# Three early attention jobs: the softmax denominator of rounds 1, 3 and 5 taken by the ones matmul from both key tiles, without the pair sum on VectorE

## The chip, the cores and the metric

The kernel runs on one core of a Trainium2 chip. The metric is the device time of one execution in microseconds (us). A core has a matrix engine (TensorE, PE in the profile; its weight loads are listed apart as PEld), VectorE (DVE), ScalarE (ACT), GpSimd (POOL) and a queue that issues the DMAs (SP). They run at the same time and wait for each other through semaphores. Each engine carries out its own instructions in the order of the program.

## What is computed

One transformer layer on 2048 tokens of width 1024, 32 heads of 32, and a feed-forward of width 3584, in bf16:

```python
scores = jnp.einsum("bhqd,bhkd->bhqk", q, k) * scale
p = _softmax(scores, axis=-1)
o = jnp.einsum("bhqk,bhkd->bhqd", p, v)
...
h = x + _A_ref(_layernorm(x, axis=-1), A_wqkv, A_wo)
h2 = h + _B_ref(_layernorm(h, axis=-1), B_w1, B_b1, B_w2, B_b2)
```

`_A_ref` is the attention with its projections, and `_B_ref` is the feed-forward with a tanh gelu. The change touches only the sum under the softmax, the denominator.

## The kernel before

**Jobs and rounds.** A job (class `Job`, L817) is 256 queries (`qb`, 0 to 7) of one group of four heads (`g`, 0 to 7), so there are 64 jobs. A job runs over the 2048 keys in eight rounds of two key tiles of 128. In each round, `qk` (L783) issues eight matmuls that put the scores of four heads and two key tiles into four PSUM banks (L796). ScalarE takes the exponential of them in two instructions of 128x1024 (L807) into a bf16 buffer `PT`. `pv` (L826) multiplies `PT` with `V` in eight matmuls (L833). These add into the first half of one PSUM bank that belongs to the job. No maximum is subtracted.

**The denominator.** It is made by a matmul with a matrix of ones, `den` (L856, matmuls at L862), which adds into the second half of the job's bank. In rounds 0 to 6, VectorE first adds the two key tiles of the round (L848, 128x1024) into a buffer `PS`, so that `den` has four matmuls. In round 7 the tile pair is taken directly: eight matmuls, and no add. There are three `PS` buffers (`NS = 3`), used in turn. An add writes a buffer only after the `den` that read it last. A `den` is issued after the `pv` of the next round. When a job is complete, `finish` (L870) has VectorE take both halves out of the bank (L878 and L885), and so frees the bank for the next taker.

**Banks.** PSUM has eight banks. Six serve the scores, in three units of two. The other two, 6 and 7, are handed out by the planner: each goes to an attention job, or to one background output (a projection or a feed-forward block) at a time. Background matmuls are recorded at L556, L559 and L562, and their results are taken out by VectorE (for instance L681, L733 and L752).

**The lead.** At the start, while tokens are still being normalized, transposed and projected, the kernel already runs scores and exponentials of three jobs, `qb` 0, 1 and 2 of head group 0 (`NLJ = 3`, L1078 to L1100). These are the lead jobs. Their 24 rounds go to buffers that stay filled: eight of the nine regular `PT` buffers and sixteen extra ones, `PX`, that lie in places that are used for something else later (K and V of other groups, and projection weights). Their `pv` and `den` come only when all keys and the V of group 0 are there. Their adds on VectorE wait for the last VectorE task of the lead (`after=hold`, L849). Background outputs that come after the key projections of group 1 wait for the end of that stage (`gate`, `late`).

**Order.** No order is written by hand. All work is put into a graph of tasks with costs, and a planner (`schedule`, L121) plays the execution forward and writes down each engine's order. On VectorE the ready task with the lowest priority number goes first: a pair sum has -2, the taking out of a finished job's bank has -1, and the taking out of a projection has 0. On TensorE (`pick_pe`, L1210) scores go first, then a closing `den`, then `pv` and `den` when enough rounds wait, and then background work. The planner counts 0.60 us for an add (`c_dve(1024, 2)`), 0.22 us for a direct `den` and 0.11 us for one from `PS`. The orders that it writes down are then fixed in the program, and the chip runs them with semaphores. A changed task can therefore alter the order of everything that is planned after it.

## Time and profile before

| | us |
|---|---|
| median of 3 runs | 1084.93 |
| lowest, highest | 1082.6, 1089.91 |
| the profiled execution | 1087.09 |
| its span in the profile | 1085.3 |
| TensorE busy (matmuls) | 1045.5 (96%) |
| ScalarE busy | 1014.5 (93%) |
| VectorE busy | 755.3 (70%) |
| exponentials into `PT`, L807, x992 | 924.5 |
| exponentials into `PX`, L807, x32 | 31.2 |
| pair sums, L848, x434 | 287.8 |
| ones matmuls from `PS`, L862, x1792 | 127.1 |

Matmuls overlap, so TensorE's busy time is not its share of peak. The mean duration of an instruction includes its pipeline. The distance from one start to the next is shorter, and is what counts when instructions follow one another without a gap. Numbers such as 62.49 in the rows are the start in us from the beginning of the span, and the second number is the time that the merged group took. Brackets behind a row give the idle time before it and who ended it.

### The profile page before, as it was taken

The numbers are of one execution on the slowest core, as the hardware profiler recorded it, in microseconds if no ns is written. First come the engines' busy times: TensorE is split into PE (matmuls) and PEld (weight loads), VectorE is DVE, ScalarE is ACT, GpSimd is POOL, SyncE is SP. The second block draws the span as 40 slices with busy tenths as digits, with TensorE's granted clock in tenths as the row PEclk, the third lists the DMA queues.
The fourth block names the chain that finished last, engine by engine and source line by source line (L and its number), as shares of the span: only waits on it lengthen the run. The fifth ranks groups of instructions, "written<-read, shape, count | busy, mean of one in ns | idle before, by whom it ended". The sixth has DMA issues, their size and how long they took to land.

```text
span 1085.3 us, 41670 instructions
## 1 busy us (share of the span) xinstructions
PE 1045.5 (96%) x18957; PEld 608.6 (56%) x19014; DVE 755.3 (70%) x1447; ACT 1014.5 (93%) x1116; POOL 43.2 (4%) x110
## 2 busy tenths in 40 slices
PE   8999999998899999999999999999999999899998
PEld 6566555554344754574475457447546744464483
DVE  8786666566586896698499669848966967686401
ACT  4999999999999999999999999999999999999650
POOL 4200000000010001001000100100010001000100
PEclk9999999999999999999999999999999999899999
DMA  8661444438464645654764565476466556866260
GB/s 221 168 163 35 145 143 120 137 118 291 161 171 147 200 164 193 231 179 147 260 220 159 206 232 177 149 258 217 159 209 233 176 191 209 248 226 236 77 244 20
DMA packets 136177, 196.37 MB, mean 181 GB/s; under 512 B 49216, under 2 KB 100288, under 8 KB 133184
## 3 DMA queue, kind: packets, MB, share of 16 engines
q1 hardware_dynamic: 136000, 193.70, 54.1%
q8 instruction: 149, 2.44, 0.9%
q14 instruction: 28, 0.23, 0.1%
HBM read 177.94 MB, written 27.26 MB: 189 GB/s over the span
## 4 chain that ended last, share of the span: by engine, by line
ACT 65%; PE 30%; DVE 3%; issue 1%; POOL 0%; POOLq 0%; DVEq 0%
ACT PT L807 60%; PE ps L559 8%; PE ps L562 6%; PE ps L556 6%; PE ps L796 4%; ACT uu L1014 3%; PE ps L833 3%; ACT PX L807 2%; PE ps L862 2%; DVE PS L848 1%; PE ps L1055 1%; PE ps L629 0%; DVE uu L1013 0%; ACT xnT L636 0%; DVE hch L1037 0%
## 5 line engine op out<-in xcount | busy, mean ns | idle before, releaser
L807 ACT ACTIVATE PT<-ps 128x1024 bf16<-128x1024 f32 x992 | 924.5, 1085 | 11.4 <-PE ps L796 10.5
L848 DVE TENSOR_TENSOR PS<-PT 128x1024 bf16<-128x1024 bf16 x434 | 287.8, 685 | 122.5 <-ACT PT L807 63.1
L796 PE MATMUL ps<-QT,KT 32*128 32x256 bf16 x4096 | 204.8, 274 | 8.0 <-ACT PT L807 6.3
L833 PE MATMUL ps<-PT,V 128*32 128x256 bf16 x3968 | 176.8, 274 | 3.4 <-ACT PT L807 3.2
L796 PEld LDWEIGHTS ps<-QT,KT 32*128 32x128 bf16 x4096 | 60.8, 92 | 162.4 <-ACT PT L807 135.9
L862 PE MATMUL ps<-PS,ones 128*32 128x256 bf16 x1792 | 127.1, 276 | 3.5 <-DVE PS L848 2.5
L559 PE MATMUL ps<-hnT,a_w1r 128*128 128x256 bf16 x979 | 119.1, 273 | 1.9 <-DVE hch L1037 1.1
L833 PEld LDWEIGHTS ps<-PT,V 128*32 128x32 bf16 x3968 | 102.1, 97 | 33.5 <-issue 6.7
L559 PEld LDWEIGHTS ps<-hnT,a_w1r 128*128 128x128 bf16 x979 | 90.1, 98 | 27.0 <-issue 15.9
L556 PE MATMUL ps<-a_w2r,gT 128*32 128x512 bf16 x1380 | 100.8, 381 | 0.6 <-DVE gT L1016 0.4
L559 PE MATMUL ps<-a_w2r,gT 128*128 128x512 bf16 x390 | 96.2, 380 | 2.8 <-issue 1.9
L556 PE MATMUL ps<-hnT,a_w1r 128*32 128x256 bf16 x2356 | 84.3, 275 | 3.3 <-issue 1.8
L992 DVE TENSOR_TENSOR gT<-ps,b1f 128x512 bf16<-128x512 f32 x98 | 67.3, 687 | 17.0 <-PE ps L559 8.9
L1037 DVE SCALAR_TENSOR_TENSOR hch<-ps,hch 128x512 bf16<-128x512 f32 x32 | 22.0, 688 | 72.3 <-PE ps L562 47.1
L556 PEld LDWEIGHTS ps<-hnT,a_w1r 128*32 128x32 bf16 x2356 | 58.6, 97 | 18.0 <-issue 15.9
L862 PEld LDWEIGHTS ps<-PS,ones 128*32 128x32 bf16 x1792 | 48.0, 97 | 28.5 <-DVE PS L848 10.2
L559 PEld LDWEIGHTS ps<-a_w2r,gT 128*128 128x128 bf16 x411 | 35.3, 98 | 46.9 <-issue 12.5
L559 PE MATMUL ps<-xnT,Wall 128*128 128x512 bf16 (+1 forms) x259 | 54.6, 344 | 2.3 <-issue 1.0
L1014 ACT ACTIVATE uu<-uu 128x1024 bf16<-128x1024 bf16 x49 | 55.3, 1129 | 0.0
L556 PEld LDWEIGHTS ps<-a_w2r,gT 128*32 128x32 bf16 x1380 | 30.5, 96 | 26.0 <-issue 16.2
L613 POOL CAST mvb<-mv 128x2 bf16<-128x2 f32 (+1 forms) x25 | 5.0, 210 | 983.1 <-DVE mv L610 983.1
L878 DVE STREAM_TRANSPOSE OD<-ps 128x256 f32<-128x256 f32 x64 | 28.5, 446 | 13.7 <-PE ps L862 6.7
(91 smaller groups left out, 1017.8 us busy)
## 6 DMA issues: line engine op xcount, KB each, us to landing
a_w2r<-w_blocks SPq DMA_DIRECT2D x105, 512.0 KB, 5.8
a_w1r<-w_blocks SPq DMA_DIRECT2D x98, 512.0 KB, 3.6
wov<-wo_blocks SPq DMA_DIRECT2D x16, 1024.0 KB, 4.9
w_blocks<-in_B_w_dram SPq DMA_DIRECT2D x28, 512.0 KB, 3.9
b_w1r<-w_blocks SPq DMA_DIRECT2D x14, 512.0 KB, 4.0
a_w1r<-in_A_wqkv_dram SPq DMA_DIRECT2D x11, 512.0 KB, 4.7
Wall<-in_A_wqkv_dram SPq DMA_DIRECT2D x17, 256.0 KB, 4.2
xrb<-in_A_x_dram SPq DMA_DIRECT2D x16, 256.0 KB, 4.8
```

The source lines that it names most:

```text
L556: fns.append(lambda p, j=j: p.matmul(psum[32 * j:32 * j + 32, bi(bank), c0:c1], lhsT[:, 32 * j:32 * j + 32], rhs, start=start, stop=stop, ...
L559: t.whole = lambda p: p.matmul(psum[:, bi(bank), c0:c1], lhsT, rhs, start=start, stop=stop, skip_group_check=True)
L562: t = pe(lambda p: p.matmul(psum[:, bi(bank), c0:c1], lhsT, rhs, start=start, stop=stop), occ, reads=reads, writes=[bb(bank)], mode="full" ...
L796: return p.matmul(psum[:, 2 * us[h // 2] + h % 2, 256 * i:256 * i + 256], KT[32 * h:32 * h + 32, g, k0:k0 + P], QT[32 * h:32 * h + 32, qs, :],
L807: act(lambda a, u=u, k=k: a.activation(PTs[s][:, k, :, :], psum[:, 2 * u:2 * u + 2, :], ACT.Exp, bias=0.0, scale=SCALE), 1024, reads=[B_ps ...
L833: fns.append(lambda p, i=i, h=h: p.matmul(psum[32 * h:32 * h + 32, bi(bank), 0:256], V[:, g, 2 * r + i, 32 * h:32 * h + 32], PTs[s][:, h / ...
L848: dve(lambda v: v.tensor_tensor(PS[:, n, :, :], pairs[:, :, 0:256], pairs[:, :, 256:512], ALU.add), c_dve(1024, 2), reads=B_PTs[s], writes ...
L862: fns.append(lambda p, h=h, rhs=rhs, i=i: p.matmul(psum[32 * h:32 * h + 32, bi(bank), 256:512], ones32[:, :], rhs, start=False, stop=last, ...
L878: t = dve(lambda v: v.transpose(OD[:, o, 1, :], psum[:, bi(bank), 256:512]), 0.36, reads=[self.B_O, self.B_D], writes=B_D, prio=-1)
L992: t = dve(lambda v: v.tensor_tensor(g[:, fc:fc + 2, :], psum[:, bi(bank), :].rearrange("p (f c) -> p f c", f=2), b1f[:, fc:fc + 2].unsquee ...
L1014: act(lambda a: a.activation(w, w, ACT.Tanh, bias=0.0, scale=KT2), 1024, reads=[B_uu[i]], writes=[B_uu[i]], prio=-1)
L1037: drop(dve(lambda v, hs=hs, bank=bank, half=half: v.scalar_tensor_tensor(hch[:, hs, c], psum[:, bi(bank), :], half, hch[:, hs, c], ALU.mul ...
```

## The change

In the three lead jobs, rounds 1, 3 and 5 are now treated as round 7 was: the round's buffer goes straight to `den`, which issues eight ones matmuls on its two tiles; no add is issued on VectorE and no `PS` buffer is taken for the round. All other jobs, and rounds 0, 2, 4 and 6 of the lead jobs, are as before.

```diff
             while self.sums:
                 self.den(*self.sums.pop(0), False)
-            if r == 7:
+            if r == 7 or self.g == 0 and self.qb < NLJ and r % 2:
                 self.sums.append((s, True))
             else:
                 n = cnt["ps"] % NS
```

## The prediction

> **What bounds the kernel now.** I read the share of each engine first, then the chain of waits that ended last, and then the lead stage in windows of 1 us and in order of time.

> ```profile
> PE 1045.5 (96%) x18957; PEld 608.6 (56%) x19014; DVE 755.3 (70%) x1447; ACT 1014.5 (93%) x1116; POOL 43.2 (4%) x110
> ACT 65%; PE 30%; DVE 3%; issue 1%; POOL 0%; POOLq 0%; DVEq 0%
> L807 ACT ACTIVATE PT<-ps 128x1024 bf16<-128x1024 f32 x992 | 924.5, 1085 | 11.4 <-PE ps L796 10.5
> ```

> ScalarE carries the chain for 65% of the span, through the exponentials of L807. Its 992 exponentials into `PT` stood idle only 11.4 us in all, mostly for scores (L796). In order of time, ScalarE runs from the first exponentials at 21.9 us to 1017.3 us, with tanh instructions in between. Then comes a tail of 68.0 us to 1085.3 (last output projection and feed-forward) that TensorE sets. So the end is the last exponential plus the tail, and the change is worth what it takes from ScalarE's idle time, or adds to it. VectorE's 70% says nothing here; what counts is the stage in which the lead jobs' adds lie. ScalarE in order of time, 50 to 125 us (the lines from 63.88 on):

> ```profile
> 63.88 7.69 ACT L807 ACTIVATE PT<-ps 128x1024 bf16<-128x1024 f32 x8
> 72.40 1.94 ACT L807 ACTIVATE PT<-ps 128x1024 bf16<-128x1024 f32 x2 [0.83 <-PE ps L796]
> 74.59 7.59 ACT L807 ACTIVATE PT<-ps 128x1024 bf16<-128x1024 f32 x8 [0.26 <-PE ps L796]
> 82.90 12.99 ACT L807 ACTIVATE PT<-ps 128x1024 bf16<-128x1024 f32 x14 [0.71 <-PE ps L833]
> 96.35 29.52 ACT L807 ACTIVATE PT<-ps 128x1024 bf16<-128x1024 f32 x32 [0.47 <-PE ps L796]
> ```

> These are four waits, 0.83 + 0.26 + 0.71 + 0.47 = 2.27 us, all for TensorE. Before them ScalarE was saturated from 30 us on. VectorE in the same stage:

> ```profile
> 59.48 3.09 DVE L848 TENSOR_TENSOR PS<-PT 128x1024 bf16<-128x1024 bf16 x5
> 62.49 5.50 DVE L848 TENSOR_TENSOR PS<-PX 128x1024 bf16<-128x1024 bf16 x9
> 67.92 0.44 DVE L878 STREAM_TRANSPOSE OD<-ps 128x256 f32<-128x256 f32 x1
> 68.28 0.38 DVE L885 COPY OD<-ps 128x256 f32<-128x256 f32 x1
> ```

> VectorE is full from 59.5 to 72.1 us. Fourteen adds stand ahead of the instructions that empty the first job's bank (L878 and L885, until 68.66), though that job's closing `den` had started at 62.34. TensorE waits for exactly that: its row at 68.72 shows the third lead job's first `pv` with an idle time of 1.28 us ended by OD L885. The windows (columns: stretch, its length, busy time of PE, PEld, DVE, ACT and POOL with counts, granted clock, DMA) show what follows:

> ```profile
> 66.00:67.00 1.00, 0.51 (x12) 0.23 (x12) 1.00 (x3) 1.00 (x3) 0.00 (x0) 1.00 0.00 0
> 67.00:68.00 1.00, 0.40 (x8) 0.12 (x8) 1.00 (x3) 1.00 (x2) 0.00 (x0) 1.00 0.00 0
> 68.00:69.00 1.00, 0.28 (x8) 0.12 (x8) 1.00 (x4) 1.00 (x2) 0.00 (x0) 1.00 0.00 0
> 69.00:70.00 1.00, 1.00 (x32) 0.66 (x28) 1.00 (x6) 1.00 (x2) 0.00 (x0) 0.78 0.08 16
> 70.00:71.00 1.00, 1.00 (x28) 0.78 (x24) 1.00 (x3) 1.00 (x2) 0.00 (x0) 0.50 0.00 0
> 71.00:72.00 1.00, 1.00 (x24) 0.41 (x16) 1.00 (x2) 0.57 (x1) 0.00 (x0) 0.50 0.25 53
> ```

> TensorE, starved by VectorE, falls to 0.28 busy, then its granted clock falls to one half until about 72.5, and ScalarE's first gap lies in that stretch.

> **Removed.** Three jobs times three rounds are 9 adds fewer, 434 to 425. One takes 685 ns, but back to back 9 take 5.50, so 0.61 each: 9 x 0.61 = 5.5 us of VectorE between 56 and 73 us. It is no term of the sum by itself; it counts through what TensorE waits for.

> **Added.** Nine `den` of eight matmuls stand in place of nine of four. In TensorE's order a four takes 0.11 us (62.23 to 62.34) and an eight 0.22 (62.34 to 62.56), so 9 x 0.11 = 0.99 us of TensorE, and 36 more weight loads of 97 ns that overlap matmuls. Their cover is TensorE's own idle time in 65 to 69 us: 4 windows less 0.93 + 0.51 + 0.40 + 0.28 busy = 1.88 us. If that cover were gone they would cost 0.99 us of background work, and ScalarE at most as much.

> **Moved.** Per pair of rounds, VectorE now needs 0.61 us, and TensorE 2 x 0.22 for `pv`, plus 0.11 and 0.22 for `den`, 0.77 us. Scores take 0.33 of each 1.84 us, so 0.77 becomes 0.94 on the clock. TensorE sets the pace instead of VectorE. The first two jobs need 8 x 0.94 = 7.5 us from 58.65, to 66.2 (before: 66.8). VectorE has their 8 adds done early, held only by the three `PS` buffers, and can empty the first bank soon after 62.3 instead of at 67.9. The third job can go on without a gap and be done near 70 (before: its last `den` at 76.6), and background work, which restarted at 73.25, near 67. The ring order later is unchanged: 21 adds became 12, both multiples of three. Buffers of odd rounds are now freed by `den` on TensorE. The first regular exponential that needs one (round 1 of the first job) comes near 66, its `den` near 59.5. The extra buffers under later projection weights are also read for the last time earlier, so the DMAs on SP that wait for them (DMA share 0.02 in 60 to 70, 0.88 in 70 to 80) can start some 2 us sooner, with what is queued behind them there. No wait is added.

> **The sum.** TensorE gains the 1.88 us and the half-clock stretch of some 3.3 us, worth 1.65, and pays 0.99: 2.5 us ahead. For ScalarE, the first two waits (0.83 + 0.26 = 1.09) go with the half clock. The third (0.71) is for a `pv` that starts at 82.44, after group 1's V was taken out at 81.56 + 0.69; this is background work that comes 2.5 us earlier, so I take it out. The fourth (0.47), scores behind 44 background matmuls, is an accident of the order, and I leave it. So -1.09 - 0.71 = -1.80, with bounds -2.27 and, if a new order gives back as much, 0. The profiled execution took 1087.09 (span 1085.3 and 1.8 around it), which becomes 1085.3. The median of the runs, 1084.93, lies 2.2 below it, so the same step gives 1083.1.

> [...]

> **The rivals.** *No half clock in most runs.* The drop may be a matter of phase in the profiled execution. Then only 0.71 is to be had: 1084.2. For it: the runs spread over 7.3 us. Against: the starvation before the drop is written into the order.

> *Given back at the hand-over.* From 262 to 300 us background work runs out: TensorE is idle 1.44 us before scores at 291.81, its clock is 0.66 in 290 to 295, and ScalarE waits 1.12 us at 295.63 (in all 2.06 us from 269 to 307). A TensorE that is 2.5 us ahead runs dry earlier and stays so longer; one or two more such stretches of 0.4 to 1.12 us take the 1.80 back: 1084.9. Against: that stretch has its waits already.

> *Slower: a redrawn order puts scores late.* After 97 us ScalarE waits 12 times, 5.94 us in all, each time for scores (L796), the longest at 295.63, 937.64 and 973.99 (1.12, 0.72 and 1.27). The planner plays on with other moments from 56 us on, and its costs have no term for a half clock. If such waits doubled, +5.94 - 1.80 = +4.1: 1089.1. It decides from the point where idle time after 97 us exceeds 5.94 + 1.80 = 7.7 us. Against: TensorE is 1 to 2.5% idle in most windows of 100 us, so not quite full, and scores have the first priority in every order.

> *More than forecast.* The new order happens to lose half of the 5.94 as well: -1.80 - 2.97 = -4.8, 1080.2. The whole is a gain of 2.27 + 5.94 = 8.2, and 10.8 only with the 2.56 us wait at 1020.17 in the tail.

> **How the numbers follow.** Forecast 0.40 (1083.1; own range 1081 to 1084.5), no half clock 0.08, given back 0.18, slower 0.24, more 0.10. One per cent, 10.8 us, is about what a measurement of this kernel can tell from no change. Within it lie the first three cases whole (0.66), 0.14 of the slower one and 0.06 of the last: 0.86. Slower by more takes some three times the present waits, 0.10; faster by more takes every wait there is, 0.04. The range leaves out the 0.10, some 0.05 of the slower case between 1090.5 and 1095.8, and of the last case what goes beyond -7 (0.05): 1078 to 1090.5.

> **What would show it.** After: 425 adds, 36 ones matmuls more; in 60 to 70 us VectorE with idle time and TensorE without; a clock of 1.00 from 66 to 73; L878 of the first job well before 67.9; background matmuls before 73.25; no wait of ScalarE in 70 to 76; the same point of the work 1.1 to 2.3 us earlier at 100 us. The forecast is wrong if the half clock stays, if the third job's bank still waits behind adds, or if idle time after 97 us grows over 7.7.

## The result, and the profile after

| | before | after |
|---|---|---|
| median of 7 runs each, us | 1085.26 | 1080.46 |
| lowest, highest | 1082.6, 1089.91 | 1078.96, 1082.41 |
| the profiled execution | 1087.09 | 1080.46 |
| its span | 1085.3 | 1078.7 |

The ratio of the times is 0.9952, with a 95% interval of 0.9935 to 0.9968. That is a gain of 4.8 us by the medians and 6.6 by the two profiled spans. A second set of runs of the changed kernel, on another chip, gave 0.9955 (0.9934 to 0.9975). The forecast was a gain of 1.8, and 1080.46 lies below its own range of 1081 to 1084.5.

The page after, with the three lines that answer to those of before:

```profile
PE 1041.8 (97%) x18987; PEld 608.7 (56%) x19044; DVE 751.5 (70%) x1438; ACT 1012.8 (94%) x1116; POOL 43.4 (4%) x110
...
ACT 74%; PE 24%; DVE 2%; issue 1%; POOL 0%; POOLq 0%
...
L807 ACT ACTIVATE PT<-ps 128x1024 bf16<-128x1024 f32 x992 | 924.5, 1116 | 7.4 <-PE ps L796 7.3
```

ScalarE carries 74% of the chain instead of 65%, and its idle time ahead of the `PT` exponentials fell from 11.4 to 7.4 us. VectorE issued 9 instructions fewer (1447 to 1438). TensorE's weight loads rose by 30, not by 36: six were saved, because the planner joined some background matmuls that it had split before (eight fewer at L556, two more at L559).

**The lead stage.** VectorE after, in order of time (start, length, line, shape):

```profile
63.05 0.69 DVE L848 TENSOR_TENSOR PS<-PX 128x1024 bf16<-128x1024 bf16 x1 [0.57 <-PE ps L862]
63.66 0.44 DVE L878 STREAM_TRANSPOSE OD<-ps 128x256 f32<-128x256 f32 x1
64.02 0.65 DVE L848 TENSOR_TENSOR PS<-PX 128x1024 bf16<-128x1024 bf16 x1
64.59 0.42 DVE L885 COPY OD<-ps 128x256 f32<-128x256 f32 x1
```

The first job's bank is empty at 65.01 us; before, it was 68.66. The adds no longer stand ahead of it: VectorE even waits 0.57 us for a `den`. TensorE's windows (stretch, length, busy time of PE, PEld, DVE, ACT and POOL with counts, granted clock, DMA) show the same six microseconds as in the prediction:

```profile
66.00:67.00 1.00, 1.00 (x44) 0.99 (x44) 0.98 (x4) 1.00 (x2) 0.00 (x0) 1.00 0.00 0
67.00:68.00 1.00, 1.00 (x40) 0.57 (x32) 1.00 (x3) 1.00 (x3) 0.00 (x0) 1.00 0.06 16
68.00:69.00 1.00, 1.00 (x44) 0.98 (x40) 1.00 (x5) 1.00 (x3) 0.00 (x0) 1.00 0.00 0
69.00:70.00 1.00, 1.00 (x40) 0.57 (x32) 1.00 (x3) 1.00 (x3) 0.00 (x0) 1.00 0.13 30
70.00:71.00 1.00, 1.00 (x28) 0.78 (x17) 0.84 (x3) 1.00 (x3) 0.00 (x0) 1.00 0.85 223
71.00:72.00 1.00, 1.00 (x22) 0.68 (x19) 0.20 (x1) 1.00 (x3) 0.00 (x0) 1.00 1.15 345
```

TensorE is full and its clock stays at 1.00. The DMA share in 70 to 72 us, 0.85 and 1.15 against 0.00 and 0.25 before, shows that the weight transfers start earlier as well. ScalarE, in order of time from 50 to 125 us, has no wait left:

```profile
60.58 4.05 ACT L807 ACTIVATE PX<-ps 128x1024 bf16<-128x1024 f32 x4
64.36 60.82 ACT L807 ACTIVATE PT<-ps 128x1024 bf16<-128x1024 f32 x66
```

Sixty-six exponentials follow one another without a gap. All four waits of before (0.83, 0.26, 0.71, 0.47) are gone.

**Where the rest came from.** ScalarE issues the same 1116 instructions in the same order in every kernel below, so its instruction numbers are marks to measure between. This table is worked out from the traces, as the distance between the starts of ScalarE's instructions 57, 123, 301, 988 and 1080 (counted from 0):

```
us from/to            start of 57   57-123  123-301  301-988  988-1080   rest     end
before                   65.71      63.89   166.03   634.60    89.95    65.12  1085.29
before, a second time    65.77      63.38   165.00   635.85    91.28    65.05  1086.33
after                    66.18      60.64   165.39   633.35    88.07    65.04  1078.67
after, a second time     66.65      60.64   166.37   634.31    87.50    65.04  1080.51
```

Two stretches are clearly shorter after: 57-123 (66 to 127 us), by 2.7 to 3.25 us, and 988-1080 (930 us to the tail), by 1.9 to 3.8. The long stretch 301-988 is shorter in both profiles too, by 0.3 to 2.5 us, but two profiles of one kernel differ there by 1.0 to 1.25; the rest overlap. The first is the stage that the change edits. The second lies some 860 us behind it. There the engines' orders are the same before and after: ScalarE's and SP's are alike throughout, and VectorE's and TensorE's differ only in what runs up to about 131 us. Two waits of ScalarE make up most of the late difference. The first is for scores near 974 us, 1.27 us before and 1.06 in the second profile of before, but none in either profile after. The second is at the start of the tail:

```profile
1020.17 0.39 ACT L882 ACTIVATE OD<-ps 128x256 f32<-128x256 f32 x1 [2.56 <-DVE OD L878]
```

This is the kernel before; the same line after is

```profile
1013.63 0.39 ACT L882 ACTIVATE OD<-ps 128x256 f32<-128x256 f32 x1 [1.44 <-DVE OD L878]
```

It is 2.97 in the second profile of before and 1.44 in the second of after. The difference is a half-clock stretch at the end of the last attention job, where TensorE has little to do. TensorE before, in windows of 2 us:

```profile
1014.00:1016.00 2.00, 1.36 (x24) 0.48 (x28) 0.86 (x2) 2.00 (x3) 0.00 (x0) 0.76 0.03 8
1016.00:1018.00 2.00, 1.67 (x14) 0.37 (x8) 0.51 (x1) 1.62 (x2) 0.00 (x0) 0.50 0.68 240
```

And after, at the same place of the work:

```profile
1008.00:1010.00 2.00, 1.18 (x28) 0.34 (x20) 0.69 (x1) 2.00 (x3) 0.00 (x0) 1.00 0.00 0
1010.00:1012.00 2.00, 1.43 (x16) 0.60 (x18) 0.69 (x1) 2.00 (x3) 0.00 (x0) 1.00 0.48 154
```

TensorE is as idle after (1.18 busy of 2.00) as before, but the clock (third number from the end) stayed at 1.00. Over the fourteen profiles of this document the wait was 1.44 us in all seven without a half clock there, and 2.36 to 3.42 us in the seven with one.

### The profile page after: what moved, and what is told of

The parts are those of the page before. It is cut to its first block, busy times and chain, and to the rows that moved or that the text cites. A ratio compares the mean times of both kernels' runs of the same rounds, so it can differ in the third digit from the quotient of the medians.

```text
span 1078.7 us, 41723 instructions
## 1 busy us (share of the span) xinstructions
PE 1041.8 (97%) x18987; PEld 608.7 (56%) x19044; DVE 751.5 (70%) x1438; ACT 1012.8 (94%) x1116; POOL 43.4 (4%) x110
## 3 DMA queue, kind: packets, MB, share of 16 engines
q8 instruction: 149, 2.44, 0.9%
## 4 chain that ended last, share of the span: by engine, by line
ACT 74%; PE 24%; DVE 2%; issue 1%; POOL 0%; POOLq 0%
ACT PT L807 67%; PE ps L559 6%; PE ps L562 5%; PE ps L556 5%; ACT uu L1014 4%; PE ps L796 3%; ACT PX L807 3%; PE ps L833 2%; PE ps L862 1%; PE ps L1055 1%; DVE PS L848 0%; PE ps L629 0%; ACT xnT L636 0%; DVE hch L957 0%; DVE st L608 0%
## 5 line engine op out<-in xcount | busy, mean ns | idle before, releaser
L807 ACT ACTIVATE PT<-ps 128x1024 bf16<-128x1024 f32 x992 | 924.5, 1116 | 7.4 <-PE ps L796 7.3
L848 DVE TENSOR_TENSOR PS<-PT 128x1024 bf16<-128x1024 bf16 x431 | 286.8, 686 | 125.8 <-ACT PT L807 65.1
L796 PE MATMUL ps<-QT,KT 32*128 32x256 bf16 x4096 | 205.0, 274 | 8.9 <-ACT PT L807 5.7
L833 PE MATMUL ps<-PT,V 128*32 128x256 bf16 x3968 | 175.7, 274 | 3.6 <-ACT PT L807 3.5
L796 PEld LDWEIGHTS ps<-QT,KT 32*128 32x128 bf16 x4096 | 61.0, 92 | 164.6 <-ACT PT L807 145.3
L862 PE MATMUL ps<-PS,ones 128*32 128x256 bf16 x1756 | 122.2, 274 | 3.0 <-DVE PS L848 2.7
L559 PE MATMUL ps<-hnT,a_w1r 128*128 128x256 bf16 x979 | 119.1, 273 | 1.7 <-DVE hch L1037 0.5
L833 PEld LDWEIGHTS ps<-PT,V 128*32 128x32 bf16 x3968 | 101.6, 97 | 33.4 <-ACT PT L807 6.3
L559 PEld LDWEIGHTS ps<-hnT,a_w1r 128*128 128x128 bf16 x979 | 90.1, 98 | 26.7 <-issue 15.7
L556 PE MATMUL ps<-a_w2r,gT 128*32 128x512 bf16 x1380 | 99.8, 381 | 0.4 <-DVE gT L1016 0.3
L559 PE MATMUL ps<-a_w2r,gT 128*128 128x512 bf16 x390 | 96.2, 380 | 2.8 <-issue 1.9
L556 PE MATMUL ps<-hnT,a_w1r 128*32 128x256 bf16 x2356 | 83.4, 276 | 1.4 <-DVE gT L992 1.0
L1037 DVE SCALAR_TENSOR_TENSOR hch<-ps,hch 128x512 bf16<-128x512 f32 x32 | 22.0, 689 | 72.1 <-PE ps L562 47.1
L556 PEld LDWEIGHTS ps<-hnT,a_w1r 128*32 128x32 bf16 x2356 | 58.5, 97 | 15.2 <-issue 11.7
L559 PEld LDWEIGHTS ps<-a_w2r,gT 128*128 128x128 bf16 x411 | 35.3, 98 | 46.9 <-issue 12.5
L559 PE MATMUL ps<-xnT,Wall 128*128 128x512 bf16 (+1 forms) x256 | 54.0, 344 | 2.4 <-issue 1.0
L556 PEld LDWEIGHTS ps<-a_w2r,gT 128*32 128x32 bf16 x1380 | 29.9, 96 | 25.7 <-issue 15.2
L878 DVE STREAM_TRANSPOSE OD<-ps 128x256 f32<-128x256 f32 x64 | 28.6, 447 | 11.5 <-PE ps L833 5.9
```

What stands on the lines that cost most here:

```text
L556: fns.append(lambda p, j=j: p.matmul(psum[32 * j:32 * j + 32, bi(bank), c0:c1], lhsT[:, 32 * j:32 * j + 32], rhs, start=start, stop=stop, ...
L559: t.whole = lambda p: p.matmul(psum[:, bi(bank), c0:c1], lhsT, rhs, start=start, stop=stop, skip_group_check=True)
L796: return p.matmul(psum[:, 2 * us[h // 2] + h % 2, 256 * i:256 * i + 256], KT[32 * h:32 * h + 32, g, k0:k0 + P], QT[32 * h:32 * h + 32, qs, :],
L807: act(lambda a, u=u, k=k: a.activation(PTs[s][:, k, :, :], psum[:, 2 * u:2 * u + 2, :], ACT.Exp, bias=0.0, scale=SCALE), 1024, reads=[B_ps ...
L833: fns.append(lambda p, i=i, h=h: p.matmul(psum[32 * h:32 * h + 32, bi(bank), 0:256], V[:, g, 2 * r + i, 32 * h:32 * h + 32], PTs[s][:, h / ...
L848: dve(lambda v: v.tensor_tensor(PS[:, n, :, :], pairs[:, :, 0:256], pairs[:, :, 256:512], ALU.add), c_dve(1024, 2), reads=B_PTs[s], writes ...
```

## The experiments

Three questions were open. Is it really the emptying of the bank behind the adds that cost the lead stage its time? What is the added TensorE work worth? Why is the late stretch shorter, although nothing in it was edited? Ratios are to the kernel before on the same chip in the same set of runs (medians 1087.99, 1088.38 and 1087.58 in the three sets, which are the first, second and third four rows), with 95% intervals; all medians are of 7 to 12 runs.

```
kernel                              median    ratio   interval
before, again                       1088.22   1.0004  0.9993-1.0015
bank first (all 21 adds)            1086.96   0.9988  0.9969-1.0008
all rounds direct (no adds)         1088.12   1.0010  0.9997-1.0023
direct matmuls, adds kept           1088.07   1.0008  0.9994-1.0022
the change, again                   1083.33   0.9955  0.9934-0.9975
the change + bank first             1084.54   0.9960  0.9944-0.9976
before, stream shifted by 72        1085.22   0.9968  0.9951-0.9984
the change, shift taken back        1088.03   1.0000  0.9987-1.0014
before, stream shifted by 256       1088.01   0.9999  0.9984-1.0015
before, stream shifted by 128       1086.70   0.9995  0.9979-1.0010
the change, shift filled to 256     1086.74   0.9995  0.9980-1.0010
bank first + shift by 72            1085.10   0.9981  0.9961-1.0001
```

### The lead stage

**The kernel before, again**, unchanged, to see what of the first profile comes back.

> The kernel before, unchanged, profiled a second time. Theory (VectorE's 14 adds ahead of the emptying of the first job's bank starve TensorE, and its clock then halves): the stretch returns, with TensorE under 0.6 busy in 66 to 69 us, a granted clock near 0.5 for some 3 us after it, and ScalarE's four waits between 70 and 97 us with at least 1.8 of their 2.27 us. Rival (the half clock was a matter of phase in one execution): no half clock there, and the waits of 0.83 and 0.26 us absent. Of the 12 later waits (5.94 us): if they belong to the order, they return at the same instructions within 0.2 us each; if they are chance, the sum differs by 1 us or more. Ratio to before 1.000 within 0.002.

The half-clock stretch came back, at 68.27 to 71.68 us instead of 69.56 to 72.97. Its windows:

```profile
67.00:68.00 1.00, 0.40 (x8) 0.12 (x8) 1.00 (x3) 1.00 (x3) 0.00 (x0) 1.00 0.00 0
68.00:69.00 1.00, 0.23 (x8) 0.14 (x8) 1.00 (x5) 1.00 (x2) 0.00 (x0) 0.63 0.00 0
69.00:70.00 1.00, 1.00 (x20) 0.27 (x16) 1.00 (x6) 0.80 (x2) 0.00 (x0) 0.50 0.07 16
70.00:71.00 1.00, 1.00 (x24) 0.72 (x21) 0.54 (x2) 1.00 (x2) 0.00 (x0) 0.50 0.00 0
```

So it is not the mark of one execution, but it does not stand at a fixed place in the program either: it is 3.41 us long in both and began at other instructions. ScalarE's waits in 60 to 97 us came to 2.00 us (2.32 in the first profile with the smallest ones counted), and its waits after 97 us to 7.23 against 6.10. The late waits of one profile differ from those of the next by about 1 us without any edit.

**Bank first**: the kernel before, with all its adds and four-part `den`, but the emptying of a lead job's bank goes ahead of the adds.

```diff
-            self.sums = []
+            self.sums, self.lead = [], g == 0 and qb < NLJ
...
-                    reads=[self.B_O, self.B_D], writes=B_D, prio=-1)
+                    reads=[self.B_O, self.B_D], writes=B_D, prio=-3 if self.lead else -1)
...
-                        reads=[self.B_O, self.B_D], writes=B_O, prio=-1)
+                        reads=[self.B_O, self.B_D], writes=B_O, prio=-3 if self.lead else -1)
```

> The kernel before with all its 21 adds, but in the three lead jobs the emptying of the bank (L878 and L885) has priority -3, ahead of the adds (-2). Theory (the held bank is what starves TensorE): the first job's bank is empty near 64 us instead of 68.7, TensorE above 0.7 busy in 66 to 69, no half clock, ScalarE's wait of 0.83 us gone; 1.5 to 3.5 us faster than before. Rival (the pace of the adds, 0.61 us each against 0.40 of TensorE's work for a round, starves TensorE wherever the bank is): TensorE goes on waiting for PS after 64 us, some of the waits stay, less than 1 us faster.

VectorE in order of time:

```profile
62.40 0.69 DVE L848 TENSOR_TENSOR PS<-PX 128x1024 bf16<-128x1024 bf16 x1
63.01 0.44 DVE L878 STREAM_TRANSPOSE OD<-ps 128x256 f32<-128x256 f32 x1
63.37 0.38 DVE L885 COPY OD<-ps 128x256 f32<-128x256 f32 x1
63.68 4.28 DVE L848 TENSOR_TENSOR PS<-PX 128x1024 bf16<-128x1024 bf16 x7
```

The bank is empty at 63.75, earlier still than after the change, with every add in place. ScalarE answers:

```profile
63.79 62.06 ACT L807 ACTIVATE PT<-ps 128x1024 bf16<-128x1024 f32 x67
```

No wait is left but 0.10 us in all, TensorE is busy 1.00, 1.00, 0.67 and 1.00 in the four windows from 66 us, and stretch 57-123 takes 60.83 us (60.64 after the change, 63.38 to 63.89 before). The bank held behind adds is the cause of the stage's loss, and the nine adds mattered only by standing in front of it. Yet the time of the whole hardly moved (0.9988, interval reaching 0.9969, where 1.5 to 3.5 us were expected): the late stretch 988-1080 stayed at 89.88 us. So the lead stage does not look like the whole gain.

**All rounds direct**: no add in the lead jobs at all, so 12 `den` more are doubled than with the change.

```diff
-            if r == 7:
+            if r == 7 or self.g == 0 and self.qb < NLJ:
```

> In the lead jobs all rounds go directly: 21 adds less than before, 21 dens of eight matmuls for four, 21 x 0.11 = 2.31 us of TensorE more than before and 1.32 more than the changed kernel. Theory (after nine adds are gone VectorE no longer holds anything up, TensorE is full): nothing more to be had; between equal to the changed kernel and 1.3 us slower than it, so 3.5 to 5 us faster than before. Rival (VectorE's time is itself what counts, 0.61 us an add): a further gain of several us, 7 or more faster than before.

ScalarE in order of time:

```profile
64.41 16.61 ACT L807 ACTIVATE PT<-ps 128x1024 bf16<-128x1024 f32 x18
82.45 43.51 ACT L807 ACTIVATE PT<-ps 128x1024 bf16<-128x1024 f32 x47 [1.43 <-PE ps L833]
```

A wait of 1.43 us is back. TensorE is full here, busy 12.00 of the 12 us from 64 to 76; its first regular `pv` starts at 81.99 us, against 79.47 with the change. The 12 doubled `den` are 12 x 0.11 = 1.32 us of it. Stretch 57-123 takes 62.31, 1.67 more than with the change. Once VectorE is out of the way, TensorE's added work counts in full, as far as one profile shows it: the sums of three rounds are taken out at no cost, those of seven are not. The expected time was missed: 3.5 to 5 us faster than before was forecast, and the ratio is 1.0010. The 1.1 to 1.6 us that the stage keeps against before do not show in the whole.

**Direct matmuls, adds kept**: TensorE's part of the change alone. The nine adds are still made, and their results are not used.

```diff
-            if r == 7:
-                self.sums.append((s, True))
-            else:
+            odd = self.g == 0 and self.qb < NLJ and r % 2
+            self.sums += [(s, True)] if r == 7 or odd else []
+            if r < 7:
...
-                self.sums.append((n, False))
+                self.sums += [] if odd else [(n, False)]
```

> As the changed kernel, with the direct dens of rounds 1, 3 and 5, but the nine adds stay on VectorE with nobody reading their result: only the matmuls of the change are in, VectorE's work is that of before. Theory (the gain comes from VectorE's adds going away ahead of the bank): the bank is emptied near 68 us again, TensorE is starved, the half clock is back; between 1 us faster and 1.5 us slower than before. Rival (the gain comes from TensorE no longer waiting for nine sums, or from the redrawn order): 3 us or more faster than before.

VectorE in order of time:

```profile
63.81 6.10 DVE L848 TENSOR_TENSOR PS<-PX 128x1024 bf16<-128x1024 bf16 x10
69.83 0.44 DVE L878 STREAM_TRANSPOSE OD<-ps 128x256 f32<-128x256 f32 x1
```

And TensorE's windows:

```profile
69.00:70.00 1.00, 0.36 (x8) 0.12 (x8) 1.00 (x3) 1.00 (x2) 0.00 (x0) 1.00 0.00 0
70.00:71.00 1.00, 0.41 (x20) 0.37 (x20) 1.00 (x4) 1.00 (x2) 0.00 (x0) 1.00 0.00 0
```

With the adds, the bank is emptied as late as before (69.83) and TensorE starves. ScalarE waits 1.90 us at 83.40, and stretch 57-123 takes 63.05, nearly as before. Here the clock did not drop, against what was expected, and the stage lost its time all the same. The starved TensorE is the cause; in the two profiles of before, where the half clock comes as well, the stretch is 0.33 and 0.84 us longer than here.

**The change with the bank first**: does the change leave anything of that kind?

> The changed kernel with the emptying of the lead jobs' banks also put ahead of the adds (priority -3). VectorE had the first bank's two instructions at 63.66 and 64.59 us in the changed kernel, with one add between them, and TensorE did not wait for them. Theory: nothing is left to gain, the same as the changed kernel within 0.0015. Rival (the add between them still delays the third job): up to 0.6 us faster at 130 us.

No: stretch 57-123 takes 61.07 us, and the ratio is that of the change. **The change, again**, ran beside it:

> The changed kernel, unchanged, on the chip and in the rounds of the other three runs. In the profiles so far the lead stage is worth about 3 us at 130 us, in the changed kernel and in the one that only empties the bank first; the latter ended 1.3 us faster (0.9988), the changed kernel 4.8 (0.9952) on another chip. Theory 1 (the stage is all that the change gives, the rest was chance of the chip): ratio 0.997 to 0.999. Theory 2 (something more is in the changed kernel than in that one): 0.994 to 0.9965 again. At 130 us ScalarE 2.5 to 3.3 us ahead of the kernel before in both.

It repeated the gain, with the first stretch at 60.64 and the last at 87.50.

### The late stretch: where TensorE's instruction stream is cut

"Bank first" and the change have the same lead stage but differ by 0.3% (0.9988 and 0.9955, intervals that overlap a little). The profiles held one more difference. TensorE before, in order of time:

```profile
969.98 1.37 PE L556 MATMUL ps<-hnT,a_w1r 128*32 128x256 bf16 x43
972.45 1.16 PE L556 MATMUL ps<-hnT,a_w1r 128*32 128x256 bf16 x33 [1.11 <-issue]
```

After the change, the same 76 matmuls:

```profile
966.02 2.25 PE L556 MATMUL ps<-hnT,a_w1r 128*32 128x256 bf16 x76
```

Before, TensorE stops for 1.11 us between the 43rd and 44th matmul, and the profile shows nothing that it waited for ("issue"). ScalarE's wait of 1.27 at 973.99 follows. Sixteen such stops of more than 0.35 us in four profiles ("before, again", bank first, all direct, adds kept) (those with every TensorE instruction on record) were placed by the number of TensorE instructions (a matmul and its weight load are two) that come after them:

```
before, again: 22657, 22144, 18560, 13952, 2432     mod 256: 129, 128, 128, 128, 128
bank first:    22140, 18556, 14715, 2428            mod 256: 124, 124, 123, 124
all direct:    24904, 15431, 2375                   mod 256:  72,  71,  71
adds kept:     25539, 14788, 11204, 4548            mod 256: 195, 196, 196, 196
```

In each kernel the stops lie whole multiples of 256 instructions apart, to within one. The page of the profile names a DMA queue for instructions:

```profile
q8 instruction: 149, 2.44, 0.9%
```

These are 149 packets of 16 KB (2.44 MB). If the 256 instructions from border to border fill one packet, each has 64 bytes; this is an estimate from these two numbers. At that size the 37,971 matmuls and weight loads on record in before come to 2.43 MB, nearly all that the queue moved. With adds kept, a packet ran from 744.86 to 745.82 and TensorE stopped from 745.13 until

```profile
747.09 0.40 PE L556 MATMUL ps<-hnT,a_w1r 128*32 128x256 bf16 x7 [1.95 <-issue]
```

TensorE went on 1.26 us after the packet's end, and in all sixteen cases 1.20 to 1.52 us after one. The packets of the stops came late: taking packets and borders in their order, 15 of the 16 began 2.5 to 3.8 us after the border before, where half of the others began within 1.2 us. The profile names no releaser at a stop; that TensorE waits there for its instructions is the author's reading of these numbers. Fourteen of the sixteen fall in the long rows of four-part matmuls of L556, which take some 30 ns each (76 in 2.25 us). So a second theory stood beside "chance": the change lengthens TensorE's stream by 61 instructions (60 for 30 more matmuls with their weight loads, and one on a semaphore), which moves every later border, and so which matmuls meet one. Counted by weight loads, the three stops in the first profile of before lie at 129 modulo 256, and the two in that of the change at 189 and 190. The next runs shift the stream by splitting or joining the 80 warm-up matmuls at its very start (L1055), which leaves all orders as they are. The written stream of the work after the warm-up is the kernel's own.

**Before, shifted by 72** (36 warm-up matmuls in two halves):

```diff
-        pe(lambda p: p.matmul(psum[:, 6, 0:256], ident[:, :], b2t[:, 0:256], start=True, stop=True), 0.18 if k < 42 else 0.115,
+        pe(lambda p, cs=[(0, 128), (128, 256)] if k > 43 else [(0, 256)]: [p.matmul(psum[:, 6, i:j], ident[:, :], b2t[:, i:j], start=True, stop=True) for i, j in cs][-1], 0.18 if k < 42 else 0.115,
```

> The kernel before, with 36 of the 80 warm-up matmuls of 256 columns split in two of 128. TensorE's instruction stream is 36 matmuls and 36 weight loads longer ahead of all later work, as it is in the changed kernel after its lead stage; all orders are as before. The gaps of TensorE that nothing in the trace explains (issue, up to 1.95 us, at 746, 925 and 972 us) lie beside 16 KB packets of the queue that brings instructions. Theory (where these gaps fall depends on the place of the instructions in the stream, and the changed kernel shifted it to better places): 1.5 to 3 us faster than before, with later gaps at other points of the work than in the kernel before. Rival (the gaps are chance): ratio 1.000 within 0.0015.

TensorE at the same matmuls:

```profile
968.46 0.39 PE L556 MATMUL ps<-hnT,a_w1r 128*32 128x256 bf16 x7
970.78 2.14 PE L556 MATMUL ps<-hnT,a_w1r 128*32 128x256 bf16 x69 [1.93 <-issue]
```

The stop has moved from behind the 43rd matmul to behind the 7th: 36 matmuls, 72 instructions, exactly the shift. The time fell by 0.32% (0.9968, 0.9951 to 0.9984), with no edit to any work that counts. But this profile does not show the gain where the theory had it: the stop is there, longer than before. What is shorter is stretch 57-123 (62.10 us) and the wait at the tail (1.44). In 57-123 TensorE starved as before, and no half clock followed (the profile of "before, shifted by 256", below, has no half clock there either and 62.38 us, at an unchanged time, so this part is not the work of the cut):

```profile
68.00:69.00 1.00, 0.06 (x4) 0.00 (x0) 1.00 (x4) 1.00 (x2) 0.00 (x0) 1.00 0.00 0
69.00:70.00 1.00, 0.66 (x16) 0.24 (x16) 1.00 (x5) 1.00 (x2) 0.00 (x0) 1.00 0.00 0
```

**The change with its shift taken back** (36 warm-up matmuls fewer, joined in pairs; in all 61 - 72 = -11 instructions against before), with the warm-up line

```diff
+        pe(lambda p, n=256 if k < 8 else 512 * (k % 2): p.matmul(psum[:, 6, 0:n], ident[:, :], b2t[:, 0:n], start=True, stop=True) if n else None, 0.18 if k < 42 else 0.115,
```

> The changed kernel with 72 of the 80 warm-up matmuls of 256 columns merged into 36 of 512, so that TensorE's instructions after the lead stage lie where they lie in the kernel before; orders are those of the changed kernel. Theory (part of the changed kernel's gain is the shift): only the lead stage's gain is left, about as the kernel that empties the bank first, 0.998 to 0.9995. Rival (no such part): the same ratio as the changed kernel in this call, within 0.0015.

The gain was gone (1.0000, 0.9987 to 1.0014). The lead stage kept its own (60.61). The stop near 970 us was back, 1.09 us long, behind the 48th matmul (43 + 11/2). This kernel has a flaw as a control, though. At 41 us, long before the lead jobs' `pv`, TensorE waited for a transposed tile:

```profile
41.06 0.62 PE L562 MATMUL ps<-Wall,xnT 128*128 128x128 bf16 x8 [1.20 <-DMA xnT<-xb]
```

It cost ScalarE 0.87 us there, and ScalarE's instruction 57 came at 67.77 instead of 66.18 to 66.65.

**Three more shifts.** Before, shifted by a whole packet (128 matmuls more, in pieces of 64 and 128 columns), should change nothing if the border counts:

> The kernel before with 128 more warm-up matmuls and weight loads by splitting, 256 instructions: one whole 16 KB packet if an instruction has 64 bytes. TensorE's unexplained gaps lay 256 instructions, or multiples, apart in every profile, so the packets' borders come to lie where they lie in the kernel before. Theory (the place matters): no change, 1.000 within 0.0015. Rival (the splitting of the warm-up itself, or a longer stream, is what made the shifted kernel faster): 0.9955 to 0.998.

The packets rose from 149 to 150, the time stayed (0.9999), and the stop was where it had been:

```profile
969.07 1.37 PE L556 MATMUL ps<-hnT,a_w1r 128*32 128x256 bf16 x43
971.27 1.16 PE L556 MATMUL ps<-hnT,a_w1r 128*32 128x256 bf16 x33 [0.83 <-issue]
```

Before, shifted by half a packet (64 matmuls more):

> The kernel before with 64 more warm-up matmuls and weight loads, 128 instructions: half a packet. Theory (the place matters): a time of its own, anywhere from 0.995 to 1.003, with TensorE's unexplained gaps at points of the work that the other kernels do not have, 128 instructions off those of the kernel before. Rival (place does not matter): 1.000 within 0.0015 and gaps at any point.

No stop near 970 us, but others, the longest at 215.8 (0.72 us) and 556.2 (1.20), and no gain (0.9995), which both theories allowed. The change, with 92 warm-up matmuls more, so that 61 + 184 = 245 leaves the borders 11 instructions off those of before:

> The changed kernel with 92 more warm-up matmuls and weight loads by splitting. With the change's own 61 instructions that makes 245, 11 short of a whole packet: the borders of the packets lie nearly as in the kernel before. Theory (the place matters): the shift's part of the gain is lost, the lead stage's is kept: 0.9965 to 0.9995, and at 130 us still 2.5 us or more ahead of the kernel before, counted from the 57th instruction of ScalarE. Rival (the place does not matter, the merged warm-up of the realigned kernel cost it its gain otherwise): 0.994 to 0.9965 as the changed kernel.

```profile
967.51 1.48 PE L556 MATMUL ps<-hnT,a_w1r 128*32 128x256 bf16 x48
969.93 0.95 PE L556 MATMUL ps<-hnT,a_w1r 128*32 128x256 bf16 x28 [0.94 <-issue]
```

The stop is behind the 48th matmul again, though the stream is now longer instead of shorter, and nearly all of the gain is gone (0.9995, 0.9980 to 1.0010). It has the same early wait as the other one (0.96 us of ScalarE at 41.67), so some 1 us of the loss is the warm-up's own.

**Bank first with the shift by 72**: if the two parts add, it should come to the change's time.

> The kernel before with the lead jobs' banks emptied first (all 21 adds kept) and with 36 warm-up matmuls split in two, which moves TensorE's later instructions by 72. Theory (two separate gains in the change: the lead stage, near 3 us, and the shift of the instruction stream, 3.5 us of 1088 for the shift alone): the two add up, 0.993 to 0.9965, without a single add removed. Rival (the two share one cause, or one is chance): 0.997 to 0.999.

It came to 0.9981 (0.9961 to 1.0001). The expected sum, 0.993 to 0.9965, did not come; the ratio is in the range of the rival, and it is not told apart from "bank first" alone (0.9988). Its profile is of its slowest run (1090.46, median 1085.10) and has stops of 2.26 us at 650 and 1.84 at 973.7.

**What this settles.** The stops sit on 256-instruction borders and move with a shift by exactly its size. Counted by weight loads, which are complete in every profile, this holds for all 46 stops of the fourteen profiles, within 3 instructions, and each time TensorE went on 1.20 to 1.58 us after a packet's end. The change loses its gain when its borders are put back, by a shorter stream as by a longer one (1.0000 and 0.9995, against 0.9952, 0.9955 and 0.9960 with its own borders), less about 1 us that is these controls' own early wait. In the kernel before, 72 instructions gave -0.32%, and 256 and 128 nothing, though those two split warm-up matmuls as well (in part others, and in part into smaller pieces). With the bank first, 72 gave no clear gain. So the place of the cut makes a difference to the time in the change and, by one shift, in the kernel before; its size is not the same in every kernel. No run shifted the kernel before by the change's own 61.

**What stays open**: through which places the time comes. The stops are a part: those over 0.35 us add up to 0.5 to 1.5 us in the three profiles with the change's own borders and to 1.7 to 5.4 in the other eleven, but to 3.4 in "before, shifted by 72", which was faster as well. The stop near 970 is absent in the same three profiles, but also in "adds kept", whose borders lie 68 instructions off those of before (196 - 128), as those of "bank first + shift by 72" do (72 - 4), which has it. And the half clock at the tail was there in seven of the fourteen profiles (both of before, the change with its borders put back in both ways, before shifted by 256 and by 128, bank first shifted) and absent in the other seven. Whether the cut decides it, or only the moment at which TensorE runs low, is not shown. Half clocks are not most of the gain: over all runs of the second set the mean granted clock was 0.9916 before, 0.9928 shifted by 72 and 0.9931 with the change. By the line through the runs of before (last section) this goes with 0.8 and 1.0 us, of 3.5 and 5.1 between the means.

## Why the prediction was right, and where its size failed

- **What holds the lead stage.** Right. The bank behind the adds, the starved TensorE, the half clock and ScalarE's waits stand in that order in two profiles of before, and the first of them alone, taken away by "bank first", takes all the others with it. The half clock is not a needed link: TensorE starves without it, and ScalarE waits.
- **Removed.** The nine adds are gone, but the counts were misread: the row of 434 is only part of L848, which was 448 in all and is 439 now, as 431 from `PT` and 8 from `PX`. As the prediction had it, they were worth nothing by themselves.
- **Added.** The nine doubled `den`, 0.99 us of TensorE, stayed hidden. What is beyond that cover is shown by "all rounds direct": 1.32 us more work, 1.67 later.
- **Moved.** The first two jobs were done at 67.15, no earlier than before (predicted 66.2, before 66.8). The third's last `den` came near 73.6 (70; before 76.6), and background work restarted at 70.27 (67; before 73.25), each with about half of the gain foreseen. TensorE set the pace as predicted, but VectorE was full as well in 67 to 70 us, and background matmuls came in between. The transfers on SP began 2 us sooner, as said.
- **The sum.** -1.80 was the step that failed, in its size. TensorE came ahead as forecast (its first regular `pv` at 79.47 instead of 82.44, 3.0 us for 2.5), and the third wait was rightly taken out. The fourth, 0.47, left in as an accident of the order, went too. And each wait was counted by its idle time alone. In that stage of before, back-to-back exponentials start 0.90 us apart although each lasts 1.07 on average; after a wait that overlap is missing. From start to start the four waits cost 1.07, 0.37, 0.88 and 0.58, in all 2.90 us instead of 2.27. So the stage gave 2.7 to 3.25 us, above the upper bound of 2.27.
- **What lies after 97 us** was treated as a matter of a redrawn order. That was the second failure. The order is redrawn only up to 131 us and then falls back into the old one; the late part gained some 2 us or more all the same (1.9 to 3.8 in the profiles). The term that was missing, as far as the shifts show it, is the length of TensorE's stream: 61 instructions more move every border behind them. That the wide range of 1078 to 1090.5 took this part in as well is luck; nothing in the sum stood for it.
- **The rivals.** "No half clock in most runs" is half true, and its price was too low. Of five profiles with the order of before, three have the half clock in the lead stage (both of before, and shifted by 128) and two do not (shifted by 72 and by 256). In those two, waits of 0.61 and 0.47 us stayed and the stretch took 62.10 and 62.38 us, so the change had some 1.5 to 1.7 to gain there without any half clock, not 0.71. "Given back" did not come to 1.80: the waits in 269 to 307 us were 2.06 and 1.46 us in the two profiles before, 1.74 and 2.60 after. "Slower": idle time after 97 us, predicted decisive beyond 7.7, was 4.39 and 5.39 us (6.10 and 7.23 before). "More than forecast" had the right number, 1080.2 against 1080.46, for a reason that does not hold: the late order is the old one.

## What to carry to other kernels

Look for the short instruction that frees a resource behind a row of long ones; moving two such instructions ahead (63 instead of 68 us) did for this stage what taking out nine adds did (60.83 and 60.64 us for stretch 57-123). Here a shift of TensorE's stream by 72 instructions alone went with a gain of 0.32%, and the change kept at most 0.05% of its 0.45 to 0.48 when its borders were put back, about 1 us of that loss being these controls' own early wait. So where an edit changes how many instructions an engine issues, run a control that adds the same number of harmless instructions to the old kernel (none here had exactly that number). And a stage's gain is better read between two fixed instructions of the bounding engine than from the whole time, where runs of one unchanged kernel spread over 7 to 11 us.
